# A squared-ReLU MLP on one core: the order of the first loads and of the first transposes

## The chip, the core and the metric

The kernel runs on one NeuronCore of a Trainium2 chip. A core has a matrix engine (PE, with its weight loads shown apart as PEld), a vector engine (DVE), a scalar engine (ACT), GpSimd (POOL) and SyncE (SP); each runs its own list of instructions and waits for the others by semaphores. SP, ACT and POOL also request transfers between HBM and the on-chip memory. All transfers of a core are carried by 16 DMA engines[...]. The metric is device time in microseconds.

## The reference

```
h   = x @ w1 + b1          # x [2048, 576], w1 [576, 4608]
h   = relu(h) ** 2
out = h @ w2 + b2          # w2 [4608, 576]
```

Everything is bf16 in memory; sums are in fp32.

## The kernel before, in words

The 2048 rows of x are four blocks of 512 (`b`), the 4608 hidden features are 36 tiles of 128 (`ft`). Phase A computes h transposed: for each block and feature tile it sums over the 576 input features, ACT adds the bias and applies ReLU (line 159), DVE squares (line 161). Phase B multiplies by w2 (line 299) and writes the rows out. The order on every engine is written out by hand.

The 576 input features are nine chunks of 64. Line 175 multiplies chunks of 64 rows: for a pair of feature tiles `j`, one tile uses the lower 64 rows of the array and the other the upper 64, nine matmuls each, so that a pair is 18 matmuls. The weights for this, `w1h`, are therefore in two halves: the lower partitions hold w1 for the first tile of each pair, the upper partitions for the second. They are loaded by line 99 in groups of four pairs. SP requests the lower halves and POOL the upper ones. The first group (pairs 2 to 5) is in two pieces for each half (320 and 256 KB on SP, 256 and 320 KB on POOL), the next three groups (pairs 6 to 9, 10 to 13, 14 to 17) are one request of 576 KB for each half, and the last two pairs (0 and 1, called at line 229) one of 288 KB. Block 0 goes through the groups in this order, from line 254 on. For the first group, line 256 does five of the nine steps for all four pairs, with only the first piece of the lower half and both pieces of the upper half, and line 258 the other four steps.

Before that, feature tiles 0 to 3 of block 0 are computed with all 128 rows of the array, so that the kernel has something to do early. This opening stage needs x's rows 0 to 511 as four row tiles `xs` (144 KB each, line 92; 0 and 2 by SP, 1 and 3 by ACT), the first 512 columns of w1 as four pieces `qn` (128 KB each, line 95) and w1's last 64 rows for these columns, `qr`, the remainder rows (two requests of 32 KB, line 110). PE transposes x against an identity (line 144), ACT and DVE copy the transposes from PSUM to `xT[0]` (lines 135 and 137, and 147 for the remainder), and `full_mm` (line 190) multiplies. It does so in two halves of 256 rows: row tiles 0 and 1, then 2 and 3. Line 213 adds the remainder rows, and lines 215, 216 and 220 copy parts of `xT[0]` to the other 64 partitions for phase A proper. The bias b1 is loaded as rows by POOL (line 116) and turned by PE (line 208).

A transfer requested by SP or ACT takes one of eight semaphores in turn, and the ninth and later ones wait until the earlier user of that semaphore has landed. In the built program line 110 waits so for row tiles 1 and 0 of x.

Of the kernel before, what the change touches and what calls it, by code (L numbers as in the profile page):

```python
# [11 lines left out]
BF16 = mybir.dt.bfloat16  # L12
# [5 lines left out]
def kernel(  # L18
# [9 lines left out]
    nc = tc.nc  # L28
    P = 128
    H = 64  # L30
    x2 = x.flatten_outer_dims()
    out2 = out.flatten_outer_dims()
    S, D = x2.shape
# [3 lines left out]
    NFT = F // P  # L37
    NJ = NFT // 2
    NC = D // P
    NH = D // H  # L40
    DM = NC * P
# [3 lines left out]
    HALF = SB // 2  # L45
# [4 lines left out]
    const = ctx.enter_context(tc.tile_pool(name="const", bufs=1))  # L50
# [4 lines left out]
    psum = ctx.enter_context(tc.tile_pool(name="psum", bufs=8, space=PSUM))  # L55
# [13 lines left out]
    def early(n):  # L69
        at[0] += n  # L70
        assert at[0] <= NFT * D
        return w2_sb[:, at[0] - n:at[0]]


    xT = [early(XW).rearrange("p (w s) -> p w s", s=SB) for b in range(NSB - 1)]
    xT3 = xpool.tile([P, NH, SB], BF16, name="xT3", tag="xT3")
    xT.append(xT3[:])
    xs = early(RT * D).rearrange("p (j c) -> p j c", c=D)
    qn = early(NC * 4 * P).rearrange("p (c f) -> p c f", c=NC)
    qr = early(2 * P)  # L80
# [10 lines left out]
    def load_x(eng, j):  # L91
        eng.dma_start(out=xs[:, j, :], in_=x_view[:, j, :])
# [13 lines left out]
    load_quad(nc.scalar, 3)  # L106
    load_x(nc.sync, 2)
    load_x(nc.scalar, 3)
    for h in range(2):
        nc.sync.dma_start(out=qr[h * H:(h + 1) * H, :], in_=w1[DM:D, 2 * h * P:2 * (h + 1) * P])  # L110

    ident = const.tile([P, P], BF16, name="ident")
    make_identity(nc, ident[:])
    b1_rows = const.tile([P, P], BF16, name="b1_rows")
    nc.gpsimd.memset(b1_rows[:], 0.0)
    nc.gpsimd.dma_start(out=b1_rows[0:NFT, :], in_=b1.rearrange("(ft p) -> ft p", p=P))


    w1_first = ((slice(0, 9, 2), slice(1, 8, 2)), (slice(1, 8, 2), slice(0, 9, 2)))
    for part in range(2):  # L120
        for h, eng in enumerate((nc.sync, nc.gpsimd)):
# [11 lines left out]
    def copy_psum(eng, dst, src):  # L133
        if eng is nc.scalar:
            nc.scalar.copy(out=dst, in_=src)  # L135
        else:
            nc.vector.tensor_copy(out=dst, in_=src)  # L137

    def transpose_chunk(half, c, eng):
        d0 = c * P if c < NC else D - P  # L140
        cols = slice(half * HALF, (half + 1) * HALF)
        tp = psum.tile([P, HALF], BF16, name="tp", tag="bank")
        for i in range(2):
            nc.tensor.transpose(tp[:, i * P:(i + 1) * P], xs[:, 2 * half + i, d0:d0 + P], ident[:])  # L144
        copy_psum(eng, xT[0][:, c if c < NC else 7, cols], tp[:])
        if c == NC:
            nc.vector.tensor_copy(out=xT[0][0:H, 8, cols], in_=tp[H:P, :])

    def hT_of(b, ft):
        if b < NSB - 1:  # L150
# [4 lines left out]
    b1T = const.tile([P, NFT], FP32, name="b1T")  # L155
# [31 lines left out]
    def full_mm(half, c):  # L187
        cols = slice(half * HALF, (half + 1) * HALF)
        for q in range(4):
            nc.tensor.matmul(bk0[q][:, cols], lhsT=qn[:, c, q * P:(q + 1) * P], rhs=xT[0][:, c, cols],  # L190
                             start=(half == 0 and c == 0), stop=False, skip_group_check=True)

    engs = (nc.vector, nc.scalar)
    n = 0
    for half in range(2):
        ahead = [0, NC, 1, 2, 3]
        lead = 3 if half == 0 else 2
        for i in range(lead):
            transpose_chunk(half, ahead[i], engs[n % 2])
            n += 1  # L200
        for c in range(NC):
            full_mm(half, c)
            if lead + c < NC + 1:
                transpose_chunk(half, ahead[lead + c], engs[n % 2])
                n += 1
        if half == 0:
            b1T_ps = psum.tile([P, P], BF16, name="b1T_ps", tag="bank")
            nc.tensor.transpose(b1T_ps[:], b1_rows[:], ident[:])
            nc.vector.tensor_copy(out=b1T[:], in_=b1T_ps[:, 0:NFT])
    for i in range(2):  # L210
        for h in range(2):
            rows = slice(h * H, (h + 1) * H)
# [126 lines left out]
```

## Time and profile before

| | us |
|---|---|
| median of 11 runs (lowest, highest) | 302.94 (301.54, 304.3) |
| the profiled execution's own time | 301.71 |
| its span, first to last instruction | 300.0 |
| PE busy | 287.1 (96%) |
| ACT, DVE, POOL busy | 95.0, 79.4, 6.9 |
| line 175, 1260 matmuls, on the chain that ended last | 137.45 |
| line 299, phase B's matmuls | 41% of the span |
| moved by DMA in all | 18.01 MB |

A line of groups or of a timeline names start and length in microseconds, engine, source line and operation, and ends with the idle time before and what ended it. A line of stretches gives busy time of each engine (and how many instructions), then the granted clock of PE (1.00 is full), the busy share of the 16 DMA engines and what they moved in GB/s. A line of a DMA queue gives packets, MB and the share of the 16 engines' time; q1 is SP's queue, q10 ACT's and q0 POOL's. A line of DMA issues gives what was moved, the requesting queue, how many, KB each, and microseconds from request to landing.

### The profile page before, as it was taken

What the parts mean: (1) busy time and instruction counts of PE and PEld (TensorE: products, weight loads), DVE (VectorE), ACT (ScalarE), POOL (GpSimd) and SP (SyncE); (2) the same over time, 40 slices, a digit from 0 to 9 for tenths busy, and PEclk for the clock granted to TensorE, in tenths of its full rate; (3) what the DMA queues carried; (4) which work ended last, traced back from release to release, by engine and by line L of the source; (5) the groups of instructions that cost most, each with busy time, mean ns of one, the idle gap of its engine ahead of it and who ended that gap; (6) DMA issues with size and microseconds to landing.
All of it is one profiled execution on the core that took longest, in us unless ns stands there. A gap on an engine that the chain in (4) does not pass through costs nothing.

```text
span 300.0 us, 4814 instructions
## 1 busy us (share of the span) xinstructions
PE 287.1 (96%) x2068; PEld 132.7 (44%) x2079; DVE 79.4 (26%) x195; ACT 95.0 (32%) x152; POOL 6.9 (2%) x16
## 2 busy tenths in 40 slices
PE   8539999999999999999999999999999999999996
PEld 4314444444444444444445544444444444444454
DVE  1223545445444454444441001111111111111111
ACT  2225766666666666666661000000000000000000
POOL 8000000000000000000000000000000000000000
PEclk9979999999999999999999999999999999999999
DMA  7999999600030000700000000000000000000000
GB/s 216 216 226 192 178 201 215 222 2 0 2 91 29 2 1 2 231 7 0 2 0 2 19 20 20 20 20 22 20 20 22 20 20 20 22 20 20 20 22 21
DMA packets 26021, 18.01 MB, mean 60 GB/s; under 512 B 14516, under 2 KB 25344, under 8 KB 26000
## 3 DMA queue, kind: packets, MB, share of 16 engines
q1 hardware_dynamic: 24576, 14.49, 20.7%
q0 software_dynamic: 848, 2.66, 4.0%
q10 hardware_dynamic: 576, 0.56, 0.6%
q8 instruction: 16, 0.26, 0.4%
q14 instruction: 5, 0.04, 0.0%
HBM read 11.94 MB, written 2.36 MB: 48 GB/s over the span
## 4 chain that ended last, share of the span: by engine, by line
PE 92%; DMA 6%; SPq 0%; issue 0%; DVE 0%
PE ph L175 46%; PE po L299 41%; PE pc L285 5%; DMA w1h<-in_w_dram 5%; DMA w_sb<-in_x_dram 1%; SPq L110 0%; DVE o_sb L301 0%
## 5 line engine op out<-in xcount | busy, mean ns | idle before, releaser
L159 ACT ACTIVATE r<-ph,b1T 128x512 bf16<-128x512 f32 x144 | 90.5, 685 | 54.6 <-PE ph L175 53.6
L175 PE MATMUL ph<-w_sb,w1h 64*128 64x512 bf16 x936 | 102.5, 379 | 5.2 <-DMA w1h<-in_w_dram 5.2
L175 PEld LDWEIGHTS <-w1h 64*128 64x128 bf16 x1260 | 60.6, 95 | 82.1 <-DMA w1h<-in_w_dram 5.7
L299 PE MATMUL po<-w_sb,hT 128*128 128x512 bf16 x423 | 92.9, 379 | 0.5
L299 PEld LDWEIGHTS <-hT 128*128 128x128 bf16 x432 | 42.2, 98 | 51.2 <-issue 0.4
L161 DVE TENSOR_TENSOR hT<-r 128x512 bf16<-128x512 bf16 x108 | 45.9, 426 | 61.8 <-ACT r L159 61.0
L301 DVE TENSOR_TENSOR o_sb<-po,b_bc 128x512 bf16<-128x512 f32 (+2 forms) x17 | 11.2, 660 | 116.7 <-PE po L299 109.7
L175 PE MATMUL ph<-xT,w1h 64*128 64x512 bf16 x324 | 35.1, 376 | 0.0
L299 PE MATMUL po<-w_sb,w1h 128*128 128x512 bf16 (+2 forms) x178 | 31.2, 336 | 0.1
L299 PEld LDWEIGHTS <-w1h 128*128 128x128 bf16 x180 | 16.2, 98 | 15.3
L161 DVE TENSOR_TENSOR w1h<-r 128x512 bf16<-128x512 bf16 x36 | 15.3, 426 | 19.6 <-ACT r L159 19.3
L285 PE MATMUL pc<-hT,w_sb 128*64 128x512 bf16 x108 | 15.7, 379 | 0.0
L285 PEld LDWEIGHTS <-w_sb 128*64 128x64 bf16 x144 | 8.1, 110 | 7.6 <-issue 0.4
L285 PE MATMUL pc<-w1h,w_sb 128*64 128x512 bf16 x36 | 7.9, 379 | 0.0
L190 PE MATMUL ph<-w_sb 128*128 128x256 bf16 x32 | 5.0, 288 | 1.7 <-ACT w_sb L135 1.3
L287 ACT ACTIVATE oc<-pc,b2T 128x512 bf16<-128x512 f32 x2 | 1.4, 687 | 13.7 <-PE pc L285 13.7
L295 DVE COPY o_sb<-oc 128x64 bf16<-128x64 bf16 x16 | 2.7, 172 | 9.3 <-DMA oc<-oc 9.3
L144 PE MATMUL tp<-ident,w_sb 128*128 128x128 bf16 x20 | 2.9, 248 | 1.9 <-DMA w_sb<-in_x_dram 1.8
L190 PEld LDWEIGHTS <-w_sb 128*128 128x128 bf16 x32 | 3.2, 100 | 2.6 <-issue 2.1
L99 POOL DMA_DIRECT2D w1h<-in_w_dram x6 | 4.3, 752 | 0.0
L135 ACT COPY w_sb<-tp 128x256 bf16<-128x256 bf16 x5 | 1.9, 372 | 7.4 <-PE tp L144 7.4
L137 DVE COPY w_sb<-tp 128x256 bf16<-128x256 bf16 x5 | 1.5, 291 | 8.7 <-PE tp L144 8.6
(27 smaller groups left out, 14.6 us busy)
## 6 DMA issues: line engine op xcount, KB each, us to landing
w_sb<-in_w_dram SPq DMA_DIRECT2D x6, 864.0 KB, 7.0
out_dram<-o_sb SPq DMA_DIRECT2D x15, 144.0 KB, 1.8
w1h<-in_w_dram POOLq DMA_DIRECT2D x3, 576.0 KB, 12.1
w1h<-in_w_dram SPq DMA_DIRECT2D x3, 576.0 KB, 21.2
w1h<-in_w_dram POOLq DMA_DIRECT2D x1, 320.0 KB, 7.3
w1h<-in_w_dram SPq DMA_DIRECT2D x1, 320.0 KB, 14.6
w_sb<-in_x_dram SPq DMA_DIRECT2D x2, 144.0 KB, 4.7
w_sb<-in_x_dram ACTq DMA_DIRECT2D x2, 144.0 KB, 4.9
```

Of the source, the lines that this page charges most:

```text
L99: eng.dma_start(out=w1h[h * H:(h + 1) * H, cs, j0 * P:(j0 + n) * P], in_=w1_rows[:, cs, f0:f0 + n * P])
L135: nc.scalar.copy(out=dst, in_=src)
L137: nc.vector.tensor_copy(out=dst, in_=src)
L144: nc.tensor.transpose(tp[:, i * P:(i + 1) * P], xs[:, 2 * half + i, d0:d0 + P], ident[:])
L159: nc.scalar.activation(out=r[:], in_=bk[:], func=ACT.Relu, bias=b1T[:, ft:ft + 1], scale=1.0)
L161: nc.vector.tensor_tensor(out=hT_of(b, ft), in0=r3, in1=r3, op=ALU.mult)
L175: nc.tensor.matmul(bk[h][:], lhsT=w1h[rows, c, j * P:(j + 1) * P], rhs=xT[b][rows, place(h, c), :], start=(i == 0), stop=(i == NH - 1))
L190: nc.tensor.matmul(bk0[q][:, cols], lhsT=qn[:, c, q * P:(q + 1) * P], rhs=xT[0][:, c, cols], start=(half == 0 and c == 0), stop=False, ski ...
L285: nc.tensor.matmul(pc[h * H:(h + 1) * H, :], lhsT=w2(ft, DM, D), rhs=hT_of(2 * pr + h, ft), start=(ft == 0), stop=(ft == NFT - 1))
L295: nc.vector.tensor_copy(out=o_sb[:, DM:D], in_=o_tr[pr][:, jj, h * H:(h + 1) * H])
L299: nc.tensor.matmul(po[:, 0:e - a], lhsT=hT_of(b, ft)[:, jj, :], rhs=w2(ft, a, e), start=(ft == 0), stop=(ft == NFT - 1))
L301: nc.vector.tensor_tensor(out=o_sb[:, a:e], in0=po[:, 0:e - a], in1=b2_bc[:, a:e], op=ALU.add)
```

## The change

Three things change, all at the start of the kernel.

- The two requests for the remainder rows `qr` move from SP to POOL, ahead of the bias. SP then goes from its second row tile of x straight to the lower halves of `w1h`.
- POOL reads one element of x's row tile 0 into a new tile `seen` before it requests the upper halves of `w1h`. Its requests stand behind that copy in its list.
- `transpose_chunks` replaces `transpose_chunk`: it transposes several chunks, row tile by row tile, and then copies them. The schedule of the opening stage is written out: the transposes for the second 256 rows start before the last multiplications of the first 256, and the turn of b1 moves from the middle to near the end.

```diff
-    for h in range(2):
-        nc.sync.dma_start(out=qr[h * H:(h + 1) * H, :], in_=w1[DM:D, 2 * h * P:2 * (h + 1) * P])
     ident = const.tile([P, P], BF16, name="ident")
     make_identity(nc, ident[:])
+    for h in range(2):
+        nc.gpsimd.dma_start(out=qr[h * H:(h + 1) * H, :], in_=w1[DM:D, 2 * h * P:2 * (h + 1) * P])
     b1_rows = const.tile([P, P], BF16, name="b1_rows")
     nc.gpsimd.memset(b1_rows[:], 0.0)
     nc.gpsimd.dma_start(out=b1_rows[0:NFT, :], in_=b1.rearrange("(ft p) -> ft p", p=P))
+    seen = const.tile([P, 1], BF16, name="seen")
+    nc.gpsimd.tensor_copy(out=seen[:], in_=xs[:, 0, 0:1])
...
-    def transpose_chunk(half, c, eng):
-        d0 = c * P if c < NC else D - P
+    def transpose_chunks(half, cs, engs):
+        tps = [psum.tile([P, HALF], BF16, name="tp", tag="bank") for c in cs]
+        for i in range(2):
+            for c, tp in zip(cs, tps):
+                d0 = c * P if c < NC else D - P
+                nc.tensor.transpose(tp[:, i * P:(i + 1) * P], xs[:, 2 * half + i, d0:d0 + P], ident[:])
         cols = slice(half * HALF, (half + 1) * HALF)
-        tp = psum.tile([P, HALF], BF16, name="tp", tag="bank")
-        for i in range(2):
-            nc.tensor.transpose(tp[:, i * P:(i + 1) * P], xs[:, 2 * half + i, d0:d0 + P], ident[:])
-        copy_psum(eng, xT[0][:, c if c < NC else 7, cols], tp[:])
-        if c == NC:
-            nc.vector.tensor_copy(out=xT[0][0:H, 8, cols], in_=tp[H:P, :])
+        for c, tp, eng in zip(cs, tps, engs):
+            copy_psum(eng, xT[0][:, c if c < NC else 7, cols], tp[:])
+            if c == NC:
+                nc.vector.tensor_copy(out=xT[0][0:H, 8, cols], in_=tp[H:P, :])
...
-    engs = (nc.vector, nc.scalar)
-    n = 0
-    for half in range(2):
-        ahead = [0, NC, 1, 2, 3]
-        lead = 3 if half == 0 else 2
-        for i in range(lead):
-            transpose_chunk(half, ahead[i], engs[n % 2])
-            n += 1
-        for c in range(NC):
-            full_mm(half, c)
-            if lead + c < NC + 1:
-                transpose_chunk(half, ahead[lead + c], engs[n % 2])
-                n += 1
-        if half == 0:
-            b1T_ps = psum.tile([P, P], BF16, name="b1T_ps", tag="bank")
-            nc.tensor.transpose(b1T_ps[:], b1_rows[:], ident[:])
-            nc.vector.tensor_copy(out=b1T[:], in_=b1T_ps[:, 0:NFT])
+    b1T_ps = psum.tile([P, P], BF16, name="b1T_ps", tag="bank")
+    V, A = nc.vector, nc.scalar
+    transpose_chunks(0, (0, 1, NC), (V, A, V))
+    full_mm(0, 0)
+    transpose_chunks(0, (2,), (A,))
+    full_mm(0, 1)
+    transpose_chunks(0, (3,), (V,))
+    full_mm(0, 2)
+    transpose_chunks(1, (0, 1), (V, A))
+    full_mm(0, 3)
+    transpose_chunks(1, (NC,), (V,))
+    full_mm(1, 0)
+    transpose_chunks(1, (2,), (A,))
+    full_mm(1, 1)
+    transpose_chunks(1, (3,), (V,))
+    nc.tensor.transpose(b1T_ps[:], b1_rows[:], ident[:])
+    full_mm(1, 2)
+    nc.vector.tensor_copy(out=b1T[:], in_=b1T_ps[:, 0:NFT])
+    full_mm(1, 3)
```

The number of matmuls, transposes, copies and bytes stays the same, but for the one-element copy.

## The prediction

> **What bounds the kernel now.** I read the chain that ended last first. After the opening it is PE without a break, so only what stands before PE's unbroken run can be won or lost.
>
> ```profile
> 4.85 14.64 DMA w1h<-in_w_dram
> ...
> 19.54 137.45 PE ph L175 x1260
> ```
>
> PE's run (line 175) starts at 19.54, when SP's first lower piece (320 KB, requested at 4.85) has landed. The stretches show what that wait costs (columns: us, then PE, PEld, DVE, ACT, POOL busy, PE clock, DMA share, GB/s):
>
> ```profile
> 7.00:9.00 2.00, 0.19 (x1) 0.10 (x1) 0.20 (x1) 0.00 (x0) 0.81 (x2) 1.00 1.02 199
> 9.00:14.40 5.40, 3.64 (x30) 2.24 (x29) 1.99 (x5) 1.35 (x4) 0.00 (x0) 1.00 1.04 211
> 14.40:19.50 5.10, 0.00 (x0) 0.00 (x0) 1.96 (x5) 2.19 (x4) 0.00 (x0) 0.93 1.05 248
> 19.50:22.30 2.80, 2.76 (x14) 1.05 (x16) 0.00 (x0) 0.00 (x0) 0.00 (x0) 0.51 1.15 198
> 22.30:30.00 7.70, 7.70 (x74) 3.43 (x72) 2.29 (x6) 3.77 (x7) 0.00 (x0) 1.00 1.15 191
> ```
>
> PE idles from 14.35 to 19.54, and then runs at half clock until about 22.25, which costs half of 2.71, 1.36 us. The DMA engines are full all the time: the start is bound by transfers. Who gets them is in the queues' lines, first of 14 to 16 us, then of 20 to 22:
>
> ```profile
> q0 software_dynamic: 112, 0.40, 77.9%
> q1 hardware_dynamic: 112, 0.11, 27.0%
> ```
>
> ```profile
> q1 hardware_dynamic: 382, 0.39, 113.6%
> ```
>
> POOL's queue (q0) and SP's (q1) get the same number of packets, but POOL's are 3.6 KB and SP's 1 KB. While POOL has work, SP moves 0.055 MB/us, alone 0.194. Together they move 256 GB/s, each alone about 200 (the rows above, 9 to 14.4 being nearly POOL alone).
>
> **When the next data are due.** A pair costs (137.45 - 1.36)/70 = 1.94 us, a group of four 7.78, the first five steps of four pairs 4.3. So PE begins the second group at 19.54 + 7.78 + 1.36 = 28.68. Its lower half was requested by SP at about 6.3:
>
> ```profile
> w1h<-in_w_dram SPq DMA_DIRECT2D x1, 576.0 KB, 19.2
> ```
>
> It landed at 25.5, 3.2 us before it was needed. That slack is all that an earlier start can use before PE meets the next wait, unless this request lands earlier too.
>
> **The change part by part.**
>
> *Remainder rows.* SP loses two requests, each 0.6 us, and its first lower piece goes out at 3.60, not 4.85; by the built program it waits for row tile 1 of x, as line 110 did. In the queue, too, two small transfers that landed 7.1 and 9.1 us after their requests (10.7 and 13.3) no longer stand ahead of it. POOL gains the two requests:
>
> ```profile
> 1.75 0.69 POOL L116 DMA_DIRECT2D b_rows<-in_b_dram  x1 [0.30 <-POOL b_rows L115]
> 2.42 4.30 POOL L99 DMA_DIRECT2D w1h<-in_w_dram  x6
> ```
>
> At 0.7 each they delay the bias and everything behind it by 1.4 us. The bias lands at 5.5 + 1.4 = 6.9 and is wanted by PE at about 9. The remainder, requested at 1.3, should land near 5.5 (the bias took 3.7 us) and is wanted at about 10.
>
> *The copy of one element.* It waits for row tile 0, there at 0.74 + 2.7 = 3.44. POOL reaches it only after identity (1.30), two requests (2.7), memset and bias request (3.9). So the wait costs nothing; the copy itself is not in the trace, and the nearest row is a 128x1 memset of 0.09 us; I allow 0.05 to 0.4 and take 0.2. Behind it on POOL stand only the upper halves and the two small requests for b2. The first upper piece goes out at 4.1 instead of 2.42. If row tile 0 came late, all of these would slip with it.
>
> *What that does to the queues.* POOL's main stream appeared in the queue about 2.8 us after its first request (2.42, then 5.2). [...] I take the row: 4.1 + 2.6 = 6.7. Row tiles 2 and 3 landed at 8.8 and 9.1 because POOL's packets came in at 5.2; by 5.2 about 1.03 of the 1.11 MB of x and `qn` had been moved, so now they land at about 6.3 (5.8 to 7). Then SP has about 1.3 us with POOL silent: 0.2 MB. POOL's 2.65 MB took 5.2 to 18.7, so now they take until 20.2. In those 13.5 us SP moves 13.5 x 0.055 = 0.74 MB. SP's requests up to the second group's lower half are 320 + 256 + 576 KB = 1.18 MB; the missing 0.24 at 0.194 take 1.2 us, to 21.4. The same reckoning of before (0.39 MB by 18.9, then 0.79 at 0.194) ends at 23.0, and the landing was 25.5[...]. Hence 24.0 (22.5 to 25.5). First lower piece: about 10.7. Second lower piece: about 16.3. Upper ones: before plus 1.5, so 10.1, 12.0 and 15.2.
>
> [...] The rows differ, 256 GB/s for both queues against 200 for one. The change replaces time in which POOL ran almost alone by time in which both run. [...]
>
> *Transposes.* The opening's second half cost 8.81 to 14.35, with four gaps of about 0.4 before `full_mm` because each transpose's copy was waited for; now a multiplication of 0.43 lies over each copy. From x at 6.5: eleven transposes and turns at about 0.08, five `full_mm` at 0.43, line 213 at 0.5, and some 0.9 of ends and bubbles make 4.5, so PE is through at 11.0 (10.4 to 12). The first piece is there at 10.7. PE starts line 175 at 11.0, 8.5 us sooner, and does not cool down there.
>
> *Where it stalls next.* Five steps to 15.3, a wait for the second lower piece to 16.3, four steps to 19.7. Then the second group, at 24.0: 4.3 us idle. Later groups are due 7.8 us apart and SP alone brings one in 3 us, so nothing after waits. The gain is therefore 28.68 - 24.0 = 4.7; the opening's finer order hides wholly under this wait, and without the wait would be worth 8.9 us.
>
> *Sum.* Of the profiled execution 301.71 - 4.7 = 297.0, span 295.3. The median was 1.2 above the profiled one: 302.94 - 4.7 = 298.3.
>
> **Clock.** [...] here 5.2 us idle gave half clock from 18.84 for 3.4 us. [...] I leave it out of the likeliest sum.
>
> **The rivals.**
>
> *Stall with cold clock* (0.17): 298.3 + 1.4 = 299.7. For it: the stall of before did so. Against: it is shorter.
>
> *The bandwidth rule holds* (0.13): the second group lands at 25.5 as before, gain 3.2, 299.8; with the clock lost as well 301.1. For it: the same bytes and full DMA engines.
>
> *The second group is not late* (0.12): if SP gets more than its packet for a packet, only PE's work binds, second group at 11.0 + 7.8 = 18.8 to 21, gain 7.7 to 9.9, 293 to 295. Against: equal packet counts at 14 to 16.
>
> *The change does nothing that lasts* (0.05): 302 to 304. The early start is used up by stalls. It would need the second group at 28 or more.
>
> *Slower: GpSimd is held up in issuing* (0.05). [...] POOL's requests now lie later, beside the DVE copies of 4 to 9 us. [...] It decides from a request later than 28.7 - 9.9 = 18.8. Against it: POOL's requests beside DVE copies took 0.68 to 0.78 in this trace.
>
> **How the numbers follow.** The likeliest has 0.48: 298.3, its own range 297.0 to 299.3. The range 294.5 to 301.2 adds the cold clock, the bandwidth rule and part of the faster case. Less than 0.3% (0.9 us) from no change is what a measurement can't tell. Faster: 0.48 + 0.17 + 0.13 + 0.12 = 0.90, less a little for sums near the edge, 0.89; same 0.06; slower 0.05.
>
> **What would show it.** SP's first lower request at 3.6; POOL's at about 4.1 with no idle before the copy; row tile 2 at about 6.3; line 175 from about 11 with clock 1.00; a new wait of line 175 for `w1h` of some 4 us, ending near 24; then PE unbroken to the end. Wrong would be: line 175 beginning after 16, more than two waits of it for `w1h`, or the new wait ending outside 22 to 26.

## The result, and the profile after

The changed kernel takes 299.84 us (median of 12 executions, 296.36 to 300.69), the kernel before 302.98 (47 executions). The ratio is 0.988, with an interval of 0.9861 to 0.9899: 1.2% faster, 3.1 us. The ratios leave out one execution, of the kernel with matmuls of constants (303.63 at clock 0.988), because it lies more than 1.5% above the fastest of its kernel. The forecast was 298.3, within 294.5 to 301.2. The profiled execution took 299.89, its span is 298.1.

The chain that ended last (start, length, what), of the kernel after, at its beginning:

```profile
3.77 0.73 SPq L99
...
4.54 0.61 SPq L99
...
5.20 19.27 DMA w1h<-in_w_dram
24.47 0.05 issue
24.52 130.07 PE ph L179 x1188
154.58 15.66 PE pc L291 x144
```

Line 179 is line 175 of before, line 219 is line 213, line 305 is line 299. The unbroken run of PE now starts at 24.52, later than the 19.54 of before, but with the second group: it has 1188 matmuls, where 1260 stood, and what it waits for is SP's third request, the second group's lower half (5.20 + 19.27 = 24.47). The first group was done before that. PE's own timeline, of the same kernel:

```profile
10.77 0.61 PE L219 MATMUL ph<-w_sb 64*128 64x512 bf16 x4
12.42 7.94 PE L179 MATMUL ph<-w_sb,w1h 64*128 64x512 bf16 x72 [1.05 <-DMA w1h<-in_w_dram]
24.52 5.75 PE L179 MATMUL ph<-w_sb,w1h 64*128 64x512 bf16 x36 [4.15 <-DMA w1h<-in_w_dram]
```

The one wait of 5.18 us has become two, 1.05 and 4.15. The stretches (us, then PE, PEld, DVE, ACT, POOL busy, clock, DMA share, GB/s) show the second and what follows it:

```profile
12.40:20.30 7.90, 7.88 (x72) 3.42 (x72) 2.85 (x8) 3.70 (x8) 0.00 (x0) 1.00 1.05 261
20.30:24.50 4.20, 0.07 (x2) 0.00 (x0) 2.09 (x5) 2.24 (x4) 0.00 (x0) 1.00 1.13 214
24.50:28.40 3.90, 3.88 (x22) 1.47 (x24) 0.00 (x0) 0.24 (x1) 0.00 (x0) 0.56 1.32 192
28.40:34.00 5.60, 5.60 (x56) 2.52 (x54) 2.55 (x6) 3.56 (x6) 0.00 (x0) 1.00 1.04 193
```

The second group starts at 24.52 where before, by the prediction's sum, it started at 28.68: 4.16 earlier. Then half clock, from 24.97 to 28.38, takes 1.7 back (half of 3.41). Phase A ends 2.41 earlier (154.58 against 19.54 + 137.45 = 156.99), which agrees. The spans differ by 1.9; the other 0.5 lies behind the last DVE operation, which ends 2.4 earlier (295.1 against 297.5) with the way out of the last rows taking that much longer in this execution.

### The profile page after: what moved, and what is told of

Its sections match the earlier page's. It is cut to its first block, busy times and chain, and to the rows that moved or that the text cites. A ratio compares the mean times of both kernels' runs of the same rounds, so it can differ in the third digit from the quotient of the medians.

```text
span 298.1 us, 4817 instructions
## 1 busy us (share of the span) xinstructions
PE 286.7 (96%) x2068; PEld 133.4 (45%) x2079; DVE 79.5 (27%) x196; ACT 94.8 (32%) x151; POOL 8.1 (3%) x19
## 3 DMA queue, kind: packets, MB, share of 16 engines
q1 hardware_dynamic: 24416, 14.42, 20.2%
q0 software_dynamic: 912, 2.73, 3.6%
## 4 chain that ended last, share of the span: by engine, by line
PE 90%; DMA 7%; SPq 0%; issue 0%; DVE 0%
PE ph L179 44%; PE po L305 42%; DMA w1h<-in_w_dram 6%; PE pc L291 5%; DMA w_sb<-in_x_dram 1%; SPq L99 0%; DVE o_sb L307 0%
## 5 line engine op out<-in xcount | busy, mean ns | idle before, releaser
L179 PEld LDWEIGHTS <-w1h 64*128 64x128 bf16 x1260 | 61.6, 95 | 81.6 <-DMA w1h<-in_w_dram 6.2
L133 PE MATMUL wps<-const-bfloat16-1.0 128*128 128x512 bf16 x6 | 2.7, 623 | 0.8 <-PEq L329 0.8
```

What stands on the lines that cost most here:

```text
L133: nc.tensor.matmul(wps[:], lhsT=ones[:, 0:P], rhs=ones[:], start=(i == 0), stop=(i == NWARM - 1))
L179: nc.tensor.matmul(bk[h][:], lhsT=w1h[rows, c, j * P:(j + 1) * P], rhs=xT[b][rows, place(h, c), :], start=(i == 0), stop=(i == NH - 1))
```

## The experiments

All ratios are against the kernel before on the same chip, with the interval in brackets. Theory A throughout: the start is bound by transfers, and what moves the time is when SP's lower halves land in a queue that shares the engines with POOL's. Theory B is the rival that each expectation names.

### The transposes alone

The kernel before with `transpose_chunks` and its written-out schedule.

```diff
-    for half in range(2):
-        ahead = [0, NC, 1, 2, 3]
...
+    transpose_chunks(0, (0, 1, NC), (V, A, V))
+    full_mm(0, 0)
+    transpose_chunks(0, (2,), (A,))
...
```

> The new order of transposes alone; remainder rows on SP, no copy of one element. Theory A (the wait for SP's first lower piece is the bound, and SP gets a packet for a packet of POOL): PE is done with the opening earlier (about 13 instead of 14.35), but line 175's matmuls begin at 19.5 as before: 303.0, within 0.8. Theory B (the finer order of the opening is a good part of the gain): 301.5 or less.

Measured: 303.09, ratio 1.0005 (0.9989 to 1.0021). PE's timeline of this kernel:

```profile
14.96 0.79 PE L217 MATMUL ph<-w_sb 64*128 64x512 bf16 x4
20.09 25.11 PE L177 MATMUL ph<-w_sb,w1h 64*128 64x512 bf16 x206 [4.35 <-DMA w1h<-in_w_dram]
```

Nothing is gained, as theory A has it. Only "done by 13" was wrong: row tile 2 came at 9.26, and from then on PE was slow, so the opening ended at 15.75. Four of its matmuls took 1.06 us there, where they take 0.60 at full clock in the changed kernel; the mean clock of this execution is 0.977. The finer order hides wholly under the wait for the first lower piece, 4.35 us.

### The remainder rows alone

```diff
-        nc.sync.dma_start(out=qr[h * H:(h + 1) * H, :], in_=w1[DM:D, 2 * h * P:2 * (h + 1) * P])
...
     make_identity(nc, ident[:])
+    for h in range(2):
+        nc.gpsimd.dma_start(out=qr[h * H:(h + 1) * H, :], in_=w1[DM:D, 2 * h * P:2 * (h + 1) * P])
```

> The two requests for the remainder rows by POOL alone; old transposes, no copy of one element. Theory A: SP's first lower piece lands at about 12.4 as in the changed kernel, the old opening ends at about 13.4, the first group at 21.2, and the second group begins at about 24.5 as in the changed kernel: 298.3 to 300.3, all of the gain. Theory B: the opening's order is needed too, 301 or more.

Measured: 300.3, ratio 0.9902 (0.9864 to 0.9941), an interval that overlaps that of the whole change. Its PE timeline:

```profile
14.27 7.93 PE L175 MATMUL ph<-w_sb,w1h 64*128 64x512 bf16 x72
24.67 20.68 PE L175 MATMUL ph<-w_sb,w1h 64*128 64x512 bf16 x190 [2.47 <-DMA w1h<-in_w_dram]
```

With the old transposes the first group starts 1.85 later than in the changed kernel and the second at the same time, 24.67. The old opening only shortens the second stall, to 2.47, and in this execution (298.38, the shortest of five) the clock stayed at 1.00 behind it. This part alone gives the gain, within what these runs tell.

### Without the copy of one element

```diff
-    seen = const.tile([P, 1], BF16, name="seen")
-    nc.gpsimd.tensor_copy(out=seen[:], in_=xs[:, 0, 0:1])
```

> The changed kernel without the copy of one element. Theory A (POOL reaches the copy when row tile 0 is already there): POOL's first upper request moves by about 0.2 us only, 299.8, within 0.8. Theory B (holding back POOL is what gave SP its lead): the first lower piece lands later than 14 and the time rises to 301 or more.

Measured: 298.77, just under the range, ratio 0.9876 (0.9852 to 0.99), the same as with it. POOL's timeline, first of the changed kernel, then without the copy:

```profile
3.13 0.53 POOL L116 DMA_DIRECT2D b_rows<-in_b_dram  x1 [0.29 <-POOL b_rows L115]
3.65 0.20 POOL L120 COPY seen<-w_sb 128x1 bf16<-128x1 bf16 x1
3.77 4.25 POOL L99 DMA_DIRECT2D w1h<-in_w_dram  x6
```

```profile
3.65 4.29 POOL L99 DMA_DIRECT2D w1h<-in_w_dram  x6
```

The copy has no idle time ahead of it, and it moves POOL's requests by 0.12 us. In this execution the first lower piece landed at 13.9, later than the 12.4 of the changed kernel and just short of theory B's bound of 14; the second group still began at 24.43, and the time didn't move.

### The remainder rows back on SP, the rest of the change kept

```diff
-    for h in range(2):
-        nc.gpsimd.dma_start(out=qr[h * H:(h + 1) * H, :], in_=w1[DM:D, 2 * h * P:2 * (h + 1) * P])
...
     load_x(nc.scalar, 3)
+    for h in range(2):
+        nc.sync.dma_start(out=qr[h * H:(h + 1) * H, :], in_=w1[DM:D, 2 * h * P:2 * (h + 1) * P])
```

> The changed kernel with the remainder rows back on SP; POOL is held by the copy until row tile 0 is there (about 3.6), so its upper requests go out when they do in the changed kernel. Theory A (the small requests ahead of it in SP's queue cost the first lower piece some 4 us beside POOL): it lands at 16 to 17.5, the first group ends near 25 to 26 with half clock in it, and no second stall is left: 299.5 to 301.5. Theory B (only the delay of POOL matters): like the changed kernel, first piece by 13.5, stall near 24.5.

Measured: 299.04, just under the range, ratio 0.9862 (0.9824 to 0.9901). Here the copy does wait (1.10 us), so POOL asks at 3.65, near the 3.77 of the changed kernel. From the timeline, a line of POOL and one of PE:

```profile
3.53 0.18 POOL L120 COPY seen<-w_sb 128x1 bf16<-128x1 bf16 x1 [1.10 <-DMA w_sb<-in_x_dram]
...
16.04 29.12 PE L179 MATMUL ph<-w_sb,w1h 64*128 64x512 bf16 x248 [5.11 <-DMA w1h<-in_w_dram]
```

The first lower piece lands at 16.0, 3.6 later than in the changed kernel, and there is no second stall, both as theory A said. Yet the time is the same. Group one at 16.04 plus 7.8, plus 2.2 for half clock, puts the second group at 26.0 with its data there. (The 2.2 is an estimate: 202 matmuls from 16.04 on took 24.16 us, and at the pace of the kernel with the remainder rows alone, 190 in 20.68 at clock 1.00, they would take 22.0.) So whether PE waits once, late, or twice makes little difference here. This kernel differs from the one with the transposes alone (1.0005) only in the copy, which delays POOL's requests by 1.2 us. That alone moves the first lower piece from 20.1 to 16.0 and reaches the time of the changed kernel without clearing SP's queue.

### POOL's first pieces as early as before, SP's queue clear

The two things are still mixed, since requests added to POOL also delay POOL. This kernel puts them behind POOL's first two upper pieces.

```diff
-    for h in range(2):
-        nc.sync.dma_start(out=qr[h * H:(h + 1) * H, :], in_=w1[DM:D, 2 * h * P:2 * (h + 1) * P])
...
             load_w1(eng, h, 2, G, w1_first[h][part])
+    for h in range(2):
+        nc.gpsimd.dma_start(out=qr[h * H:(h + 1) * H, :], in_=w1[DM:D, 2 * h * P:2 * (h + 1) * P])
```

> The kernel before with the remainder rows requested by POOL behind its first two upper pieces, so that SP's queue is free of them and POOL's first upper requests go out at 2.4 as before. Theory A (the two small requests in SP's queue held up the first lower piece): it lands near 12.5, and the time is that of the changed kernel, about 299.8. Theory B (what POOL has already queued when SP's piece is requested holds it up): it lands at 15 or later, the second stall shrinks or goes, and the time is 299 to 301. The landing tells them apart, not the time.

Measured: 300.81, ratio 0.9895 (0.9857 to 0.9933). POOL's timeline, and of the DMA issues the first lower piece (requested at 3.69; KB, us to landing):

```profile
2.44 1.37 POOL L99 DMA_DIRECT2D w1h<-in_w_dram  x2
3.78 1.12 POOL L122 DMA_DIRECT2D w_sb<-in_w_dram  x2
```

```profile
w1h<-in_w_dram SPq DMA_DIRECT2D x1, 320.0 KB, 8.3
```

It lands at 12.0, with POOL's first pieces requested at 2.44 as before. That is the landing of theory A. But SP's piece is now requested at 3.69 and no longer at 4.85, and POOL's other four pieces go out 1.1 later, from 4.87 on, behind it. The queues, from 6 to 8 and from 8.5 to 11, show SP's piece nearly still while what POOL has queued moves, as theory B has it:

```profile
q0 software_dynamic: 111, 0.35, 91.3%
q1 hardware_dynamic: 27, 0.02, 7.5%
```

```profile
q1 hardware_dynamic: 477, 0.47, 93.8%
q0 software_dynamic: 60, 0.10, 18.8%
```

First POOL's queue moves 0.35 MB and SP's 0.02; then SP's moves 0.47 and POOL's 0.10. Over all profiles the landing of SP's first lower piece goes with how many of POOL's pieces were requested ahead of it: with four it came at 19.5 to 20.4, with two at 16.0 (small requests in SP's queue) and 12.0 (none there), with one or none at 9.4 to 13.9. So the two small requests and the order of the large ones each seem to be worth some 4 us; no run changes the first without the second.

PE lost the early landing again: the opening ran largely at half clock (0.61 from 8 to 15, 0.50 from 15 to 17) and ended at 17.0.

### Matmuls of constants in the new stall

```diff
+    wp2 = bank("wp2")
+    for i in range(16):
+        nc.tensor.matmul(wp2[:], lhsT=ones[:, 0:P], rhs=ones[:], start=(i == 0), stop=(i == 15))
     for j in range(2 + G, NJ):
         a_step(0, j)
```

> The changed kernel with 16 matmuls of constants (3.4 us, result not used) between the first and the second group, in the new stall. Theory A (the stall's second price is the half clock after it): the second group still begins at about 24.5, the clock stays at 1.00 after it, and the time falls to 298.2, within 0.7, with less spread. Theory B (the clock costs nothing lasting, or the matmuls get in the way): 299.8 or more.

Measured: ratio 0.9819 (0.979 to 0.9849), which is 297.6 at 303.07; the three executions compared lie at 296.47 to 298.27, each at clock 1.00. The fourth (303.63, clock 0.988) has no trace, and what held it up is not known. The changed kernel had 0.988 (0.9861 to 0.9899); run once more (below), on another chip, it gave 0.9876, with clock 0.988 to 0.994. The stretches around the second group, of this kernel and then of the changed kernel's second profile, in both of which the group began at 23.6:

```profile
23.50:27.00 3.50, 3.43 (x32) 1.56 (x34) 0.42 (x1) 1.26 (x2) 0.00 (x0) 1.00 1.14 200
27.00:32.00 5.00, 5.00 (x50) 2.22 (x48) 2.13 (x5) 2.98 (x5) 0.00 (x0) 1.00 1.19 184
```

```profile
23.50:27.00 3.50, 3.42 (x18) 1.24 (x20) 0.00 (x0) 0.00 (x0) 0.00 (x0) 0.50 1.14 198
27.00:32.00 5.00, 5.00 (x38) 2.04 (x36) 1.35 (x4) 2.53 (x4) 0.00 (x0) 0.74 1.15 155
```

In the 8.5 us after the stall's end the kernel with the warm matmuls does 82 matmuls (32 + 50), the other 56 (18 + 38). The 26 that are missing are 2.8 us at 0.108 each (336 in 36.43 us with the warm matmuls), and in this profile half clock lasted from about 22.7 to 29.6, twice the 3.41 us of the first; the two ratios differ by 0.57%, 1.7 us. Theory A holds in three of four executions: the half clock after the stall costs about 2 us, and the 16 matmuls whose result is thrown away paid for themselves where the engine would stand still.

### The changed kernel once more

> The changed kernel once more, on the chip of these runs, as the base for the other two: 299.8, within 0.8; executions whose granted clock is above 0.998 below 298.5, those below 0.992 above 299.

Measured: 300.22, ratio 0.9876 (0.9842 to 0.991). All four executions had clock 0.994 or less. Only one of the 16 executions of the changed kernel had more (0.999), and it is the fastest, 296.36. The three below 0.992 lie above 299, as expected; none was above 0.998, so the other half of the expectation stays untested here. One stretch of 3.41 us at half clock makes a mean clock of about 0.994 in a span of 298, two make 0.989. By that estimate nine of the 16 executions had twice 3.41 us of it, and the profile of this one shows as much: its clock is 0.91 from 19.3 to 23.5, 0.50 to 27.0 and 0.74 to 32.0, which is half clock for 6.9 us.

### POOL held back until row tile 3

```diff
-    nc.gpsimd.tensor_copy(out=seen[:], in_=xs[:, 0, 0:1])
+    nc.gpsimd.tensor_copy(out=seen[:], in_=xs[:, 3, 0:1])
```

> The changed kernel, but the copied element is of row tile 3, so that POOL really waits, until about 6.5. Theory A (SP moves 0.19 MB/us while POOL is silent and 0.055 beside it): POOL's stream begins near 8, the first lower piece lands near 9, line 175 starts at about 11.7, stalls for about 2 for the second upper piece, and the second group begins at about 22.5: 296.5 to 298.5. Theory B (the same bytes over the same 16 engines): second group at 24.5 as before this edit, 299.8.

Measured: 300.83, ratio 0.9923 (0.9898 to 0.9948): a miss, in the numbers of both theories. From the timeline, a line of POOL and one of PE:

```profile
8.11 0.19 POOL L120 COPY seen<-w_sb 128x1 bf16<-128x1 bf16 x1 [4.44 <-DMA w_sb<-in_x_dram]
...
18.02 27.32 PE L179 MATMUL ph<-w_sb,w1h 64*128 64x512 bf16 x232 [6.25 <-DMA w1h<-in_w_dram]
```

The first lower piece did land early, at 9.4 (5.7 us after its request at 3.65). But row tile 3 came at 8.1, not 6.5, and then the first upper piece took 9.7 us from its request at 8.23 to landing, where it takes 5.0 in the changed kernel. The queues show it, from 8.4 to 14.4 and from 15 to 17:

```profile
q1 hardware_dynamic: 1204, 1.20, 110.6%
```

```profile
q0 software_dynamic: 105, 0.37, 76.0%
q1 hardware_dynamic: 129, 0.12, 31.2%
```

For more than six microseconds after its request POOL's queue moves no packet at all, and then the two queues alternate. In that time SP moved 1.20 MB, by estimate about what was left of its first four requests (1.77 MB in all, moved at some 0.2 MB/us). So POOL's queue, asking late, moved only after much of what SP had queued, though not after all of it: SP's fifth request, made by 7.2, took 21.1 us to land. POOL's issuing of its first piece took 0.66 us, as in the changed kernel, so that is not what held it up. What in the hardware does this was not tried.

### The big requests dealt out anew

```diff
-    for m in range(1, 4):
-        for h, eng in enumerate((nc.sync, nc.gpsimd)):
-            load_w1(eng, h, 2 + G * m, G, slice(0, NH))
+    for eng, m, h in ((nc.gpsimd, 1, 1), (nc.gpsimd, 1, 0), (nc.sync, 2, 0), (nc.gpsimd, 2, 1), (nc.sync, 3, 0), (nc.sync, 3, 1)):
+        load_w1(eng, h, 2 + G * m, G, slice(0, NH))
```

> The changed kernel with the big requests dealt out anew: POOL takes both halves of the second group, then the upper half of the third; SP takes the lower half of the third and both halves of the fourth. Each queue moves as many bytes as in the changed kernel. Theory A (the second group waits only because its lower half stands in the queue that gets one small packet for each large one): both halves land by about 17, no stall after the first group, clock 1.00 from the start of line 175 on: 294.4, 293.6 to 295.5. Theory B (the DMA engines' total is the limit): the stall stays, 298 or more.

Measured: 293.09, half a microsecond better than the range, ratio 0.9662 (0.9621 to 0.9703), 3.4% under the kernel before and about 7 us under the changed one. The chain of its profiled execution (296.06 at clock 0.994; the other four had 0.999 or 1.00):

```profile
3.73 9.17 DMA w1h<-in_w_dram
12.89 0.05 issue
12.94 47.16 PE ph L178 x314
```

PE runs unbroken from the first lower piece on. Both queues carry as many bytes as in the changed kernel (14.42 MB for SP's, 2.73 for POOL's), and in the first three fortieths of the span all queues together move 206, 262 and 244 GB/s, in the changed kernel 209, 253 and 254; what differs is which data ride in POOL's large packets (0.63 MB in 171 packets, SP's 0.17 in 169, from 14 to 17 in the changed kernel). This settles where the rest of the change's gain went: into the wait for a lower half that stood in the queue with the smaller share (25.6% of the engines' time against 80.6%, from 14 to 17; the wait is 4.15 us) and the half clock behind it (1.7 us in the first profile, 3.0 in the second).

The same edit on the kernel before:

> The kernel before with the same dealing out of the big requests as s_swap and nothing else. Theory A: line 175 still begins at 19.5 with the first lower piece, and nothing after it was late: 303.0, within 0.8. Theory B (the dealing out is worth something by itself): 301 or less.

Measured: 303.57, ratio 1.0007 (0.9992 to 1.0021). Phase A's matmuls (line 175 of before) began at 20.42. Where the first lower piece comes at about 20, the second group is in time and dealing the requests out anew is worth nothing: it needs the earlier start, which by itself gives 1.2%.

The new dealing with seven matmuls of constants between opening and line 175:

```diff
+    wp2 = bank("wp2")
+    for i in range(7):
+        nc.tensor.matmul(wp2[:], lhsT=ones[:, 0:P], rhs=ones[:], start=(i == 0), stop=(i == 6))
     nc.vector.tensor_copy(out=xT[0][0:H, 4:7, :], in_=xT[0][H:P, 0:3, :])
```

> s_swap with seven matmuls of constants (1.5 us, result not used) in the wait between the opening and line 175's first matmul. If the one slower execution of s_swap (296.06, clock 0.994) is the half clock after that wait, it does not come back and all executions lie at 292.3 to 294.3, clock 1.00; if the wait was already short enough, no change from 293.1.

Measured: 294.09, ratio 0.9679 (0.9644 to 0.9714), clocks 0.998 to 1.00, one execution (295.18) above the range. The clock of 0.994 did not come back, but four executions against one such case don't show that the matmuls did it, and no time is gained over the new dealing alone.

## Why the prediction was right, and where it was off

*The bound and the next stall.* Right. The gain was read from the slack of the second group and not from the wait that the change removes. The second group was forecast for 24.0 and came at 24.52, the stall for 4.3 us and was 4.15, the second lower piece for 16.3 and landed at 4.54 + 11.8 = 16.3. With the second group's wait gone, in the redealt kernel, the gain is 10.2 us (3.4%) and not 3.1. The prediction has 8.9 for a start without that wait, but puts it to the transposes; it is the whole start's. The old order of transposes starts line 175 only 1.85 later.

*The transposes* were costed at nothing under the wait, and that is what they gave (1.0005). *The copy of one element* likewise; 0.20 us of POOL, as taken. POOL's six requests took 0.66 to 0.74 us each, so the rival in which GpSimd is held up in issuing did not come.

*The remainder rows.* Right that they are the effective part. But the prediction named two ways, SP's queue and POOL's delay, and gave most of its sum to the second. The runs show that the second is enough: delaying POOL with the requests left on SP gives the same time (0.9862). Clearing SP's queue gives it too (0.9895, first lower piece at 12.0, POOL's first pieces not delayed), but with POOL's later pieces behind SP's first, so it is not shown by itself.

*Sizes within the sum.* POOL's stream began about 1.7 us after its request and not 2.6, near 5.5 instead of 6.7. Row tiles 2 and 3 came at 7.6 and 7.9, not 6.3, the first lower piece at 12.4, not 10.7, and line 175 at 12.42, not 11.0: 7.1 sooner than before and not 8.5. The shares made up for it. The prediction took one SP packet for each POOL packet throughout. That held later, from 14 to 17, but not from 8 to 10. In the changed kernel, first 8 to 10, then 14 to 17:

```profile
q0 software_dynamic: 70, 0.25, 51.4%
q1 hardware_dynamic: 237, 0.23, 51.0%
```

```profile
q0 software_dynamic: 171, 0.63, 80.6%
q1 hardware_dynamic: 169, 0.17, 25.6%
```

SP moved 0.115 MB/us where 0.055 was taken. The two errors cancelled in the landing of the second group, which is luck and not reckoning.

*The clock is the term that was left out.* The prediction left half clock after the stall out of its sum; as a rival it had 0.17, at 1.4 us. By their clocks (0.987 to 0.994) 15 of 16 executions of the changed kernel had once or twice 3.41 us of it, and in both profiles it stands at the stall. In the first profile it cost 1.7. With it the sum is 298.3 + 1.7 = 300.0; measured were 299.84. That they agree so closely is in part luck, since most executions had it twice. The rival "stall with cold clock" (299.7) was the right case and its price about right; the reason against it, that this stall is shorter than the one before, was not: 4.15 us had half clock behind them as 5.18 had. Here are the stretches around the second stall, cut where the clock changes (24.97 and 28.38) and at the same length ahead of that:

```profile
18.15:21.56 3.41, 2.22 (x22) 0.78 (x16) 2.27 (x6) 3.41 (x7) 0.00 (x0) 1.00 1.08 258
21.56:24.97 3.41, 0.45 (x6) 0.22 (x8) 1.13 (x3) 0.98 (x2) 0.00 (x0) 1.00 1.12 194
24.97:28.38 3.41, 3.41 (x20) 1.23 (x18) 0.00 (x0) 0.22 (x1) 0.00 (x0) 0.50 1.36 192
```

Behind the stretch with PE busy for 0.45 of 3.41 us, 13%, comes half clock; the last section has other stalls and stretches.

*The rival named after bandwidth* kept the second group at 25.5. It began at 24.5 and, in the second profile, at 23.6; the sum from the queues' rows, with 24.0, was the better guide.

## What to carry to other kernels

When a wait at the start is removed, look up when the next data are due at PE's full pace: the gain ends at the slack of the next request, here 4.2 of the 7.1 us by which line 175 starts sooner. Which queue carries which data can be worth more than how many bytes they are: here POOL's queue, with 3.7 KB to a packet, had 80.6% of the engines' time from 14 to 17 us and SP's, with 1.0 KB, 25.6%, at 171 and 169 packets. Put what is due next in the queue with the larger share (1.2% became 3.4% here, and it was worth nothing without the earlier start). Look too at the order in which the queues are given their requests. And price each remaining wait with the half clock that can follow it: 1.7 us behind the 4.15 here, 3.0 in the second profile.

## What the runs showed of the hardware

*Half clock behind the stalls at the start.* In the profiled executions of before and of the changed kernel half clock behind the stall lasted 3.41 us (18.80 to 22.21 and 24.97 to 28.38). At clock 1.00, in the kernel with the remainder rows alone, 190 matmuls took 20.68 us, 0.109 each. At that pace the matmuls that the timelines list behind five other stalls would have been done sooner; that half clock is what made them longer is an estimate from these times and the mean clock of each execution:

| kernel | stall, us | matmuls behind it | took, us | at 0.109 each | mean clock |
|---|---|---|---|---|---|
| without the copy of one element | 3.37 | 72 | 9.23 | 7.8 | 0.994 |
| the transposes alone | 4.35 | 206 | 25.11 | 22.4 | 0.977 |
| the kernel before with the new dealing | 4.40 | 212 | 24.80 | 23.1 | 0.976 |
| the remainder rows back on SP | 5.11 | 202 | 24.16 | 22.0 | 0.988 |
| POOL held back until row tile 3 | 6.25 | 10 | 2.31 | 1.1 | 0.987 |

Behind the stalls of before (5.18) and of the changed kernel (4.15 and 4.21) the clock was 0.50. In the redealt kernel it was 0.50 behind a stall of 2.56; behind one of 2.47, with the remainder rows alone, it stayed at 1.00.

*How busy PE was ahead of it.* In the kernel with the remainder rows behind POOL's first pieces, a stretch of 3.41 us with PE busy for 52% had half clock behind it; in the kernel before, one with 54% had full clock:

```profile
6.12:9.53 3.41, 1.76 (x17) 1.20 (x16) 0.49 (x2) 0.00 (x0) 2.19 (x4) 1.00 1.06 209
9.54:12.95 3.41, 2.65 (x15) 1.72 (x14) 0.58 (x2) 0.75 (x2) 0.65 (x2) 0.50 1.09 229
```

```profile
5.15:8.56 3.41, 1.84 (x18) 1.41 (x16) 0.53 (x3) 0.37 (x1) 2.66 (x5) 1.00 1.05 242
8.56:11.97 3.41, 1.99 (x16) 1.40 (x17) 0.85 (x3) 0.74 (x2) 0.00 (x0) 1.00 1.06 202
```

In the redealt kernel 0.86 of the 3.41 us from 9.52 to 12.93 was busy, 25%, with half clock behind it. But at its last matmuls a stretch with 45% had full clock behind it:

```profile
289.40:292.81 3.41, 1.53 (x28) 1.35 (x25) 0.40 (x2) 0.00 (x0) 0.00 (x0) 1.00 0.14 43
292.82:296.23 3.41, 0.00 (x0) 0.00 (x0) 0.00 (x0) 0.00 (x0) 0.00 (x0) 1.00 0.01 2
```

So the share of busy time alone does not sort these stretches, and what does was not shown.

*One queue stood still while another moved.* With POOL held back until row tile 3, POOL's queue moved no packet from 8.4 to 14.4 us, while SP's moved 1204. With the remainder rows behind POOL's first pieces, SP's moved 0.02 MB from 6 to 8 us, while POOL's moved 0.35. In the kernel before, SP's two requests of 32 KB took 7.1 and 9.1 us to land; from 8 to 10 us SP's queue moved 0.02 MB and POOL's 0.41. Later in the same traces the two queues get about as many packets each (112 and 112 in the kernel before from 14 to 16, 105 and 129 with POOL held back from 15 to 17). Why the first stretch differs from the later one is open.
